# Expert capacities at a pitch of 8 tokens instead of 32, in a fused attention and mixture-of-experts kernel

## The chip, the cores and the metric

The kernel runs on one core of one Trainium2 chip. The metric is the time of one execution on the device, in microseconds (us). The engines are PE (TensorE, with its weight loads shown apart as PEld), DVE (VectorE), ACT (ScalarE), POOL (GpSimd) and SP (SyncE, which here only issues DMAs).

## What is computed

A windowed attention with sinks (4 batches, 8 heads, 768 positions, head size 64) gives 3072 tokens of 512 features. Each token picks one of 4 groups and one of the 4 experts in it, and goes through that expert alone:

```python
def _moe_ref(x, w_group, w_expert, w1, w2):
    ...
    g_idx = np.argmax(g_logits, axis=1)
    ...
        e_logits = xg @ w_expert[g]
        e_idx = np.argmax(e_logits, axis=1)
        ...
        for e in range(Eg):
            mask_e = e_idx == e
            if not mask_e.any():
                continue
            h = np.maximum(xg[mask_e] @ w1[g, e], 0.0)
            ye = h @ w2[g, e]
            combined = g_w[mask_g][mask_e] * e_w[mask_e]
            tok_idx = np.where(mask_g)[0][mask_e]
            out[tok_idx] = combined[:, None] * ye
```

`w1[g, e]` is 512x1024 and `w2[g, e]` 1024x512, in float32: 16 experts with 4 MB of weights each. `g_w` and `e_w` are the softmax weights of the group and the expert. How many tokens an expert gets is known only when the attention is done.

## The kernel before

The first part of the program is the attention, 128 queries at a time, with the routing worked out beside it on DVE. The second part runs the experts. They are ordered by how many tokens they hold, so an expert is named here by its **rank** r, from 0 (most tokens) to 15. A program without data-dependent loops needs a fixed number of places for each rank: the table `CAPT`. If an expert holds more tokens than its rank has places, `nov` is positive, and behind the main program a general path (`overflow`) runs the tokens that were left over, expert by expert, with nothing beside it.

Tokens are gathered from DRAM into tiles of 128 rows (`gather`), turned by PE so that features lie on partitions (`xpose`), and split into a high part, rounded to the format that PE takes in one pass (`F32R`), and a low part, the remainder. Weights are split in the same way in chunks of 128x1024: `whi` by a cast on ACT, `wlo` by a subtraction on DVE (`wjob`). A product is then three products: high by high, low by high, high by low. Both parts of the tokens stand side by side in one buffer: `xx` (before the first layer) and `hx` (before the second), the low part `T` columns behind the high part, T being the number of places.

`PARTS` lists the stages in the order in which they run (rank 0 first, then 1, 2, 2, 3 with 14, 8, 4 with 15, 9, 6 with 12, 5, 7 with 13, 10, 11). A stage has these forms:

- `layer1_wide` (T above 128): weights are stationary, tokens stream. For each of 8 blocks f of the hidden layer and 4 chunks c of the features: with T of 240 or more, three matmuls of T columns (a **triple**); below, `comb` is true and one matmul of 2T columns takes high and low together with `whi`, and one of T columns takes `wlo` (a **pair**).
- `layer1_narrow` (T up to 128): tokens are stationary, 512 weights stream; the hidden layer is then turned by PE (`hidden_t`).
- `layer2`: 128 tokens (or what is left of them) are stationary, 512 columns of `w2` stream, three matmuls for each of 8 blocks. Where the last tile holds at most 64 tokens (s > 0), its high and low parts stand next to each other and are loaded as one stationary operand.
- `few_tokens`: for the ranks in `FEW` (3, 4, 8, 9, 10, 11) the tokens above the last multiple of 128 (the **remainder**, `hq`) go through the second layer in plain float32, at 32 columns each, four matmuls side by side in the array. m is T without the remainder.
- `plain` (ranks 14 and 15): both layers in that way.

The order of all engines is fixed by the program text (`Pinned`). Between the matmuls, `spend(us)` counts an estimated time and emits weight jobs (`wjob`) and routing steps for ACT and DVE when enough of it has passed; the estimate of a block in `layer1_wide` is T/200 us and a constant. SP loads weight chunks ahead of that as buffers come free (`prefetch`). The results are scaled by ACT (`ot`) and written by an indirect DMA on POOL's queue (`scatter`).

Of the kernel before, what the change touches and what calls it, by code (L numbers as in the profile page):

```python
# [15 lines left out]
AF = mybir.ActivationFunctionType  # L16
ALU = mybir.AluOpType
# [5 lines left out]
P = 128  # L23
# [4 lines left out]
DM = H * D  # L28
# [14 lines left out]
XW = DM + GW  # L43
NEG = -1.0e30
BIG = 1 << 20
CAPT = [384, 256, 480, 288, 288, 224, 192, 192, 160, 160, 160, 160, 128, 128, 64, 32]
NTR = [(t + P - 1) // P for t in CAPT]
BASE = [sum(NTR[:r]) for r in range(NE)]
NCOL = sum(NTR)
# [19 lines left out]
MAXT = N // P  # L69
PARTS = [[dict(r=0, j0=0, T=EC * P, last=False), dict(r=0, j0=EC, T=CAPT[0] - EC * P, last=True)]]  # L70
for _g in GROUPS:
    if CAPT[_g[0]] > 3 * P:
        PARTS.append([dict(r=_g[0], j0=0, T=2 * P, last=False)])
        PARTS.append([dict(r=_g[0], j0=2, T=CAPT[_g[0]] - 2 * P, last=True)])
    else:
        PARTS.append([dict(r=r, j0=0, T=CAPT[r], last=True) for r in _g])
for _g in PARTS:
    _o = 0
    for _q in _g:
        _rem = _q["T"] % P  # L80
        _m = _q["T"] - _rem if _q["r"] in FEW else _q["T"]
        _q.update(o=_o, nt=(_q["T"] + P - 1) // P, s=_rem if _rem <= 64 and _m == _q["T"] else 0, plain=_q["T"] <= 64, m=_m)
        _o += 0 if _q["plain"] else 2 * _q["T"]
MAXB = 6
MAXA = 7
MAXO = MAXT + NE
# [48 lines left out]
def moe_attention(tc, kqT, vN, vS, nsw, wgx, w1, w2, out):  # L135
    nc = Pinned(tc)
    v = nc.vector
    with ExitStack() as top, ExitStack() as att:
# [18 lines left out]
        wz = const([P, 192], BF16, "wz")  # L157
        nc.gpsimd.memset(wz, 0.0)

        W = max(sum(2 * q["T"] for q in g if not q["plain"]) for g in PARTS)  # L160
        un = cp.tile([P, (NDC + NFC) * W], F32R, name="un")
        kb = wk.tile([P, 1 + 2 * NT, HP, BW], F32, name="kb", bufs=1)
        qb = wk.tile([P, NQ, HP, P], F32, name="qb", bufs=1)
        xx = un[:, 0:NDC * W].rearrange("p (c w) -> p c w", w=W)
        hx = un[:, NDC * W:(NDC + NFC) * W].rearrange("p (f w) -> p f w", w=W)
        dif = gp.tile([P, P], I32, name="xg")
# [146 lines left out]
        def late_consts():  # L313
# [8 lines left out]
            for r in range(NE):  # L322
                nc.gpsimd.memset(capt[:, r:r + 1], float(CAPT[r]))
                nc.gpsimd.memset(caps[:, r:r + 1], float(CAPT[r] // P))
# [151 lines left out]
        start = const([P, NE], F32, "start")  # L476
# [344 lines left out]
        po = ob[1].rearrange("p (c n) -> p c n", c=HP)  # L821
# [118 lines left out]
            v.tensor_copy(gate[0:w], src[0:w, DM:DM + 1])  # L940

        def split_h(q, fs, src):
            T, o, s, m = q["T"], q["o"], q["s"], q["m"]
            hi = hx[:, fs, o:o + m]
            nc.scalar.activation(hi, src[..., 0:m], AF.Relu)
            dve(0.1 + T / 960)
            yield
            if m < T:
                v.tensor_scalar(q["hq"][:, fs], src[..., m:T], 0.0, None, ALU.max)
            for a, z, d in ((0, m - s, m + s), (m - s, m, s)):  # L950
                if z > a:
                    v.scalar_tensor_tensor(hx[:, fs, o + a + d:o + z + d], src[..., a:z], 0.0,
                                           hi[..., a:z].bitcast(F32), ALU.max, ALU.subtract)
# [52 lines left out]
        def side_by_side(out, w, n, k, xs, ws, chunk, plain=True):  # L1006
            m = P // w
            for k0 in range(0, n, m):
                kk = range(k0, min(n, k0 + m))
                for c in kk:  # L1010
                    for a in range(m):
                        nc.tensor.matmul(out[a * w:(a + 1) * w, 0:k], xs(c), ws(c)[:, a * k:(a + 1) * k], start=c == 0, stop=c == n - 1)
                for c in kk:
                    held.pop(chunk(c), None) if chunk(c) != chunk(c + 1) else None
                prefetch(RAW + RAWB)
                if n == NFC and not plain:
                    pop_todo()
                yield 0.46 * k * m / 512 * len(kk) * w / 64
# [52 lines left out]
            yield from few_tokens(q, spare(), q["h"], q["T"], 0)  # L1071

        def few_tokens(q, po, h, T, jj):
            r, k = q["r"], DM * T // P
            yield from side_by_side(po, T, NFC, k, lambda f: h[:, f],
                                    lambda f: whole(2, r, f // 2)[:, (f % 2) * DM:(f % 2 + 1) * DM], lambda f: (2, r, f // 2), q["plain"])
            c = cg[r, jj]
            ot = yp.tile([P, DM], F32, name="ot", bufs=3)
            for a in range(P // T):
                nc.scalar.activation(ot[0:T, a * k:(a + 1) * k], po[a * T:(a + 1) * T, 0:k], AF.Copy, scale=c[0:T])  # L1080
            scatter(r, jj, T, ot)

        def scatter(r, jj, w, ot):
            cc = BASE[r] + jj
            nc.gpsimd.indirect_dma_start(
                out=outs[cc], out_offset=bass.IndirectOffsetOnAxis(ap=sidx[0:w, cc:cc + 1], axis=0),
                in_=ot[0:w], in_offset=None, bounds_check=N - 1, oob_is_err=False)

        def layer2(q, j):
            T, o, s, r, m = q["T"], q["o"], q["s"], q["r"], q["m"]  # L1090
            w = min(P, T - j * P)
            st = w if j * P + w > T - s else 0
            po = ps_o.tile([P, DM], F32, name="po")
            lastj = (j + 1) * P >= m
            end = q is PARTS[-1][-1] and j == 0
            rest = rest_of(q) if m < T and j == 0 else None
            pb = [spare(), po] if end else None
            for u, f in [(u, f) for u in range(2) for f in range(NFC)] if end else []:
                us = slice(f % 2 * DM + u * DM // 2, f % 2 * DM + (u + 1) * DM // 2)
                whi, wlo = (t[:, us] for t in weights(2, r, f // 2))  # L1100
                hh, hl = (hx[:, f, k:k + w] for k in (o, o + m + s))
                a, z = f == 0, f == NFC - 1
                nc.tensor.matmul(pb[u][:, 0:DM // 2], hh, whi, start=a, stop=False)
                nc.tensor.matmul(pb[u][:, 0:DM // 2], hh, wlo, start=False, stop=False)
                nc.tensor.matmul(pb[u][:, 0:DM // 2], hl, whi, start=False, stop=z)
                yield 0.36
                if rest and u == 0 and z:
                    yield from rest
            for f in range(0 if end else NFC):
                whi, wlo = (t[:, (f % 2) * DM:(f % 2 + 1) * DM] for t in weights(2, r, f // 2))  # L1110
                hh = hx[:, f, o + j * P:o + j * P + w]
                a, z = f == 0, f == NFC - 1
                if st:
                    hb = hx[:, f, o + j * P:o + j * P + 2 * w]
                    if z:
                        nc.tensor.matmul(po[0:w], hh, wlo, start=False, stop=False)
                    nc.tensor.matmul(po[0:2 * w], hb, whi, start=a, stop=z)
                    if not z:
                        nc.tensor.matmul(po[0:w], hh, wlo, start=False, stop=False)
                else:  # L1120
                    hl = hx[:, f, o + m + s + j * P:o + m + s + j * P + w]
                    nc.tensor.matmul(po[0:w], hh, whi, start=a, stop=False)
                    nc.tensor.matmul(po[0:w], hh, wlo, start=False, stop=False)
                    nc.tensor.matmul(po[0:w], hl, whi, start=False, stop=z)
                pop_todo()
                state["freed"] += 1 if q["last"] and lastj and f % 2 else 0
                yield 0.467 if st else 0.7
                if rest and f == 3:
                    yield next(rest)
            jj = q["j0"] + j  # L1130
            ot = yp.tile([P, DM], F32, name="ot", bufs=3)
            c = cg[r, jj]
            if end:
                for u in range(2):
                    nc.scalar.activation(ot[:, u * DM // 2:(u + 1) * DM // 2], pb[u][:, 0:DM // 2], AF.Copy, scale=c)
            else:
                nc.scalar.activation(ot[0:w], po[st:st + w], AF.Copy, scale=c[0:w])
            if st:
                v.scalar_tensor_tensor(ot[0:w], po[0:w], c[0:w], ot[0:w], ALU.mult, ALU.add)
            scatter(r, jj, w, ot)  # L1140
            if rest and not end:
                yield from rest

        def rest_of(q):
            po = spare()
            yield from few_tokens(q, po, q["hq"], 32, q["j0"] + q["nt"] - 1)

        def fetch(nxt):
            for q in nxt:
# [31 lines left out]
        for i in range(NI + 2):  # L1181
            live = i < NI
            a, b = i - 1, i - 2
# [385 lines left out]
```

## Time and profile before

| | us |
|---|---|
| median of 3 timed runs (lowest, highest) | 497.98 (496.86, 499.21) |
| the profiled execution | 493.82 |
| its span, first to last instruction | 492.0 |
| PE busy in the span | 479.8 |
| PEld / DVE / ACT / POOL busy | 412.4 / 350.8 / 331.2 / 157.2 |

The profiled execution is 1.8 us longer than its span. It lies 4.2 us (0.8%) under the median of the timed runs, which were separate executions.

### The profile page before, as it was taken

The numbers are of one execution on the slowest core, as the hardware profiler recorded it, in microseconds if no ns is written. First come the engines' busy times: TensorE is split into PE (matmuls) and PEld (weight loads), VectorE is DVE, ScalarE is ACT, GpSimd is POOL, SyncE is SP. The second block draws the span as 40 slices with busy tenths as digits, with TensorE's granted clock in tenths as the row PEclk, the third lists the DMA queues.
The fourth block names the chain that finished last, engine by engine and source line by source line (L and its number), as shares of the span: only waits on it lengthen the run. The fifth ranks groups of instructions, "written<-read, shape, count | busy, mean of one in ns | idle before, by whom it ended". The sixth has DMA issues, their size and how long they took to land.

```text
span 492.0 us, 15335 instructions
## 1 busy us (share of the span) xinstructions
PE 479.8 (98%) x5769; PEld 412.4 (84%) x5769; DVE 350.8 (71%) x1140; ACT 331.2 (67%) x878; POOL 157.2 (32%) x286
## 2 busy tenths in 40 slices
PE   8999999999999999999999999999999999999995
PEld 6788888888888888989888779797889788988894
DVE  7676888888988789973174157464788887788970
ACT  4898888889984355762264186646788777687861
POOL 3663563563573022322303042102402260105021
PEclk9999999999999999999999999999999999999999
DMA  7876767877876469894124389659959997768100
GB/s 215 248 229 225 260 228 227 253 254 263 286 254 212 131 227 387 289 316 148 68 70 142 113 291 385 208 180 329 391 180 386 399 394 238 280 212 292 61 28 28
DMA packets 50002, 114.75 MB, mean 233 GB/s; under 512 B 9486, under 2 KB 9486, under 8 KB 49920
## 3 DMA queue, kind: packets, MB, share of 16 engines
q1 hardware_dynamic: 45424, 100.14, 60.0%
q0 software_dynamic: 4352, 13.26, 7.5%
q8 instruction: 47, 0.77, 0.6%
q10 hardware_dynamic: 144, 0.29, 0.3%
q14 instruction: 35, 0.29, 0.2%
HBM read 100.89 MB, written 13.24 MB: 232 GB/s over the span
## 4 chain that ended last, share of the span: by engine, by line
PE 77%; DVE 7%; issue 7%; ACT 5%; POOL 1%; DMA 1%; POOLq 0%; DVEq 0%; ACTq 0%
PE po L105 34%; PE ph L105 28%; PE tp L105 7%; PE ps L105 6%; PE lg L105 3%; DVE wlo L105 2%; ACT pt L105 1%; ACT whi L105 1%; DVE sm L105 1%; DMA ni<-in_nsw 1%; POOL out L105 1%; DVE un L105 1%; DVE ps L105 1%; DVE xt L105 0%; ACT ot L105 0%
## 5 line engine op out<-in xcount | busy, mean ns | idle before, releaser
L105 DVE TENSOR_TENSOR wlo<-rw,whi 128x1024 fp32r<-128x1024 f32 x112 | 134.5, 1223 | 32.7 <-ACT whi L105 32.1
L105 PE MATMUL ph<-un,whi 128*128 128x256 f32 (+4 forms) x576 | 132.0, 316 | 1.4 <-DVE hc L105 0.8
L105 PE MATMUL po<-whi,un 128*128 128x512 f32 (+2 forms) x384 | 126.7, 395 | 0.0
L105 ACT CAST whi<-rw 128x1024 fp32r<-128x1024 f32 (+1 forms) x116 | 115.2, 1020 | 8.5 <-PE po L105 5.1
L105 POOL DMA_INDIRECT out<-ot,sidx x33 | 41.2, 1248 | 225.3 <-ACT ot L105 156.5
L105 PE MATMUL ph<-un,wlo 128*128 128x160 f32 (+4 forms) x416 | 100.6, 267 | 0.0
L105 PEld LDWEIGHTS ph<-un,whi 128*128 128x128 f32 x576 | 94.2, 189 | 3.8 <-DVE hc L105 1.3
L105 PEld LDWEIGHTS po<-whi,un 128*128 128x128 f32 (+1 forms) x384 | 70.8, 186 | 19.4 <-issue 2.6
L105 ACT ACTIVATE pt<-sm,st 128x136 f32<-128x136 f32 x192 | 76.0, 399 | 14.9 <-DVE st L105 14.8
L105 PE MATMUL po<-wlo,un 128*128 128x512 f32 (+3 forms) x200 | 78.0, 390 | 0.0
L105 PEld LDWEIGHTS ph<-un,wlo 128*128 128x128 f32 x416 | 77.0, 189 | 1.0
L105 DVE CUSTOM_DVE_ANT_0 sm<-ps,msk 128x136 f32<-128x136 f32 x192 | 45.7, 296 | 4.9 <-PE ps L105 1.9
L105 POOL DMA_INDIRECT xg<-xd,gidx x33 | 36.9, 1118 | 35.6 <-DVE idz L105 24.5
L105 PEld LDWEIGHTS po<-wlo,un 128*128 128x128 f32 (+2 forms) x200 | 36.3, 182 | 7.7
L105 DVE TENSOR_TENSOR hc<-ph,hc 128x160 f32<-128x160 f32 (+2 forms) x64 | 22.0, 346 | 26.4 <-ACT hc L105 26.1
L105 PE MATMUL ps<-kb,qb 64*64 64x216 f32 (+1 forms) x768 | 39.4, 339 | 0.8 <-DVE st L105 0.5
L105 ACT ACTIVATE un<-ph 128x256 fp32r<-128x256 f32 x40 | 15.4, 385 | 36.0 <-PE ph L105 35.6
L105 ACT ACTIVATION_READ_ACCUMULATOR pt<-sm,st 128x1 f32 x192 | 36.3, 189 | 0.0
L105 ACT ACTIVATE ot<-po,cg 128x512 f32<-128x512 f32 (+3 forms) x25 | 17.0, 680 | 27.6 <-PE po L105 27.5
L105 ACT COPY hc<-ph 128x160 f32<-128x160 f32 (+2 forms) x64 | 19.8, 312 | 19.0 <-PE ph L105 15.0
L105 PEld LDWEIGHTS ps<-kb,qb 64*64 64x64 f32 x768 | 26.4, 132 | 7.0 <-issue 1.0
L105 POOL TENSOR_SCALAR_AFFINE_SELECT pu<-pa 64x512 f32<-64x512 f32 x40 | 27.1, 676 | 12.0 <-ACT pa L105 11.9
(220 smaller groups left out, 737.9 us busy)
## 6 DMA issues: line engine op xcount, KB each, us to landing
rw<-in_w SPq DMA_DIRECT2D x128, 512.0 KB, 5.8
vv<-in_vN SPq DMA_DIRECT2D x24, 512.0 KB, 4.5
kb<-in_kqT SPq DMA_DIRECT2D x23, 288.0 KB, 4.5
qb<-in_kqT SPq DMA_DIRECT2D x24, 256.0 KB, 3.8
xd<-xt SPq DMA_DIRECT2D x24, 256.0 KB, 3.1
svr<-in_vS SPq DMA_DIRECT2D x4, 192.0 KB, 5.3
xg<-xd,gidx POOLq DMA_INDIRECT x33, 6.2
out<-ot,sidx POOLq DMA_INDIRECT x33, 5.8
```

The lines of the kernel that those rows point to most:

```text
L105: r = f(*a, **k)
```

## The change

Nine of the 16 ranks get fewer places: the table's numbers, multiples of 32 before, are now multiples of 8. With this case's inputs the ranks hold the numbers of tokens in the second row, counted with the reference:

| rank | 0 | 1 | 2 | 3 | 4 | 5 | 6 | 7 | 8 | 9 | 10 | 11 | 12 | 13 | 14 | 15 |
|---|---|---|---|---|---|---|---|---|---|---|---|---|---|---|---|---|
| tokens | 382 | 244 | 475 | 275 | 270 | 204 | 188 | 163 | 157 | 156 | 150 | 134 | 108 | 92 | 54 | 20 |
| places before | 384 | 256 | 480 | 288 | 288 | 224 | 192 | 192 | 160 | 160 | 160 | 160 | 128 | 128 | 64 | 32 |
| places after | 384 | 248 | 480 | 280 | 272 | 208 | 192 | 168 | 160 | 160 | 152 | 136 | 112 | 96 | 64 | 32 |

Reads of PSUM by ACT and DVE start at partitions 0, 32, 64 or 96 in this program. Rank 7's last tile now holds 40 tokens, so its low part is kept 64 columns behind the high part (`gap`), with 24 columns of it belonging to neither. Remainders of 24, 16 and 8 tokens keep their places at a pitch of 32 (`out[a * w:a * w + xs(c).shape[-1]]`).

```diff
-CAPT = [384, 256, 480, 288, 288, 224, 192, 192, 160, 160, 160, 160, 128, 128, 64, 32]
+CAPT = [384, 248, 480, 280, 272, 208, 192, 168, 160, 160, 152, 136, 112, 96, 64, 32]
...
-        _q.update(o=_o, nt=(_q["T"] + P - 1) // P, s=_rem if _rem <= 64 and _m == _q["T"] else 0, plain=_q["T"] <= 64, m=_m)
-        _o += 0 if _q["plain"] else 2 * _q["T"]
+        _s = _rem if _rem <= 64 and _m == _q["T"] else 0
+        _q.update(o=_o, nt=(_q["T"] + P - 1) // P, s=_s, gap=64 if _s else 0, plain=_q["T"] <= 64, m=_m)
+        _q["wid"] = 0 if _q["plain"] else 2 * _q["T"] + _q["gap"] - _s
+        _o += _q["wid"]
...
         def split_h(q, fs, src):
-            T, o, s, m = q["T"], q["o"], q["s"], q["m"]
+            T, o, s, m, gap = q["T"], q["o"], q["s"], q["m"], q["gap"]
...
-                v.tensor_scalar(q["hq"][:, fs], src[..., m:T], 0.0, None, ALU.max)
-            for a, z, d in ((0, m - s, m + s), (m - s, m, s)):
+                v.tensor_scalar(q["hq"][:, fs, 0:T - m], src[..., m:T], 0.0, None, ALU.max)
+            for a, z, d in ((0, m - s, m + gap), (m - s, m, gap)):
...
         def side_by_side(out, w, n, k, xs, ws, chunk, plain=True):
...
-                        nc.tensor.matmul(out[a * w:(a + 1) * w, 0:k], xs(c), ws(c)[:, a * k:(a + 1) * k], start=c == 0, stop=c == n - 1)
+                        nc.tensor.matmul(out[a * w:a * w + xs(c).shape[-1], 0:k], xs(c), ws(c)[:, a * k:(a + 1) * k], start=c == 0, stop=c == n - 1)
...
         def few_tokens(q, po, h, T, jj):
-            r, k = q["r"], DM * T // P
+            r, k, w = q["r"], DM * T // P, h.shape[-1]
...
-                nc.scalar.activation(ot[0:T, a * k:(a + 1) * k], po[a * T:(a + 1) * T, 0:k], AF.Copy, scale=c[0:T])
-            scatter(r, jj, T, ot)
+                nc.scalar.activation(ot[0:w, a * k:(a + 1) * k], po[a * T:a * T + w, 0:k], AF.Copy, scale=c[0:w])
+            scatter(r, jj, w, ot)
...
         def layer2(q, j):
-            T, o, s, r, m = q["T"], q["o"], q["s"], q["r"], q["m"]
+            T, o, s, r, m = q["T"], q["o"], q["gap"], q["r"], q["m"]
             w = min(P, T - j * P)
-            st = w if j * P + w > T - s else 0
+            st = s if j * P + w > T - q["s"] else 0
...
-                    hb = hx[:, f, o + j * P:o + j * P + 2 * w]
+                    hb = hx[:, f, o + j * P:o + j * P + st + w]
...
-                    nc.tensor.matmul(po[0:2 * w], hb, whi, start=a, stop=z)
+                    nc.tensor.matmul(po[0:st + w], hb, whi, start=a, stop=z)
```

The numbers of matmuls, weight chunks, gathers and scatters stay the same, and so does the width of the token buffers (`W` is set by rank 0). What changes in the instruction streams is the size of the tiles, and, because `spend` counts the smaller T, the places of a few weight jobs.

On PE, at the start of rank 11's first layer (`ph` is its accumulator, `un` the tokens, `hq` the remainder of rank 10 that is finished just ahead), before:

```order
L105 MATMUL ph<-rw,hq 32x128 x16
L105 MATMUL ph<-un,whi 128x320
L105 MATMUL ph<-un,wlo 128x160
L105 MATMUL ph<-un,whi 128x320
L105 MATMUL ph<-un,wlo 128x160
L105 MATMUL ph<-un,whi 128x320
L105 MATMUL ph<-un,wlo 128x160 x2
L105 MATMUL ph<-un,whi 128x320 x2
```

and now:

```order
L107 MATMUL ph<-rw,hq 24x128 x16
L107 MATMUL ph<-un,whi 128x272
L107 MATMUL ph<-un,wlo 128x136
L107 MATMUL ph<-un,whi 128x272
L107 MATMUL ph<-un,wlo 128x136
L107 MATMUL ph<-un,whi 128x272
L107 MATMUL ph<-un,wlo 128x136 x2
L107 MATMUL ph<-un,whi 128x272 x2
```

The sequence is the same; the streamed widths fall from 320 and 160 columns to 272 and 136, and the stationary remainder from 32 columns to 24.

Also on PE, where rank 7's second tile ends in the second layer and rank 13's tile begins (`po` is the accumulator, the first number the tokens that are stationary), before:

```order
L105 MATMUL po<-whi,un 128x512
L105 MATMUL po<-wlo,un 64x512
L105 MATMUL tp<-ident,xg 128x128 x4
L105 MATMUL tp<-ident,xg 128x32 x4
L105 MATMUL po<-wlo,un 64x512
L105 MATMUL po<-whi,un 128x512 x2
L105 MATMUL po<-wlo,un 128x512
L105 MATMUL po<-whi,un 128x512 x2
```

and now:

```order
L107 MATMUL po<-whi,un 104x512
L107 MATMUL po<-wlo,un 40x512
L107 MATMUL tp<-ident,xg 128x128 x4
L107 MATMUL tp<-ident,xg 128x24 x4
L107 MATMUL po<-wlo,un 40x512
L107 MATMUL po<-whi,un 104x512
L107 MATMUL po<-whi,un 96x512
L107 MATMUL po<-wlo,un 96x512
```

Again nothing has moved: 512 columns stream in each matmul as before, and the stationary operand is narrower (64 to 40, 128 to 104, 128 to 96).

On DVE, in rank 1's first layer, where the last steps of the routing run between the splits of weights (`wlo`) and of the hidden layer (`un`), before:

```order
L105 TENSOR_SCALAR inc<-inc 128x1
L105 TENSOR_TENSOR inc<-inc,gen 128x1
L105 CAST geni<-inc 128x1
L105 TENSOR_TENSOR inc<-inc 128x1
L105 TENSOR_TENSOR wlo<-rw,whi 128x1024
L105 SCALAR_TENSOR_TENSOR un<-ph,un 128x256
L105 CAST novi<-inc 128x1
L105 SCALAR_TENSOR_TENSOR un<-ph,un 128x256
L105 TENSOR_TENSOR wlo<-rw,whi 128x1024
```

and now:

```order
L107 TENSOR_SCALAR inc<-inc 128x1
L107 TENSOR_TENSOR inc<-inc,gen 128x1
L107 TENSOR_TENSOR wlo<-rw,whi 128x1024
L107 SCALAR_TENSOR_TENSOR un<-ph,un 128x248
L107 CAST geni<-inc 128x1
L107 TENSOR_TENSOR inc<-inc 128x1
L107 SCALAR_TENSOR_TENSOR un<-ph,un 128x248
L107 CAST novi<-inc 128x1
L107 TENSOR_TENSOR wlo<-rw,whi 128x1024
```

One split of a weight chunk (`wlo`) has moved ahead of two small routing steps and another behind the next two tiles; one more moves by one place in rank 4's first layer. On SP three weight loads of rank 3 now stand behind register loads (`eidi`, expert numbers) that stood between them. POOL's order is unchanged.

## Rows read from the trace of the kernel before

**Rows 1.** The page: span, busy time by engine (share of span), instructions.

```profile
span 492.0 us, 15335 instructions
...
PE 479.8 (98%) x5769; PEld 412.4 (84%) x5769; DVE 350.8 (71%) x1140; ACT 331.2 (67%) x878; POOL 157.2 (32%) x286
```

**Rows 2.** PE's waits, whole span: us in total, times, longest us.

```profile
PE tp L105 <- ACT pa L105: 1.3, 2, 0.7
...
PE ph L105 <- DVE hc L105: 0.8, 2, 0.4
```

**Rows 3.** Stretches: length; busy us PE, PEld, DVE, ACT, POOL; clock, DMA, GB/s.

```profile
225.00:250.00 25.00, 25.00 (x148) 22.26 (x147) 6.76 (x20) 7.56 (x20) 4.38 (x5) 1.00 0.18 62
...
350.00:375.00 25.00, 24.18 (x206) 21.35 (x206) 20.57 (x53) 20.22 (x46) 7.12 (x6) 1.00 0.78 288
375.00:400.00 25.00, 25.00 (x125) 20.45 (x124) 21.66 (x34) 20.12 (x31) 7.11 (x4) 1.00 1.04 396
```

**Rows 4.** PE timeline, triples: first and last of 32 (256, 288 tokens).

```profile
217.09 0.40 PE L105 MATMUL ph<-un,whi 128*128 128x256 f32 x2
...
228.09 0.40 PE L105 MATMUL ph<-un,whi 128*128 128x256 f32 x2
...
263.37 0.43 PE L105 MATMUL ph<-un,whi 128*128 128x288 f32 x2
...
275.72 0.43 PE L105 MATMUL ph<-un,whi 128*128 128x288 f32 x2
```

**Rows 5.** PE timeline, pairs: a stage's first row and the next's (224, 192, 160).

```profile
240.45 0.37 PE L105 MATMUL ph<-un,whi 128*128 128x448 f32 x1
...
250.53 0.39 PE L105 MATMUL po<-whi,un 128*128 128x512 f32 x1
...
421.02 0.34 PE L105 MATMUL ph<-un,whi 128*128 128x384 f32 x1
...
430.17 0.39 PE L105 MATMUL ph<-whi,un 128*128 128x512 f32 x1
...
452.47 0.31 PE L105 MATMUL ph<-un,whi 128*128 128x320 f32 x1
...
460.75 0.40 PE L105 MATMUL po<-whi,un 128*128 128x512 f32 x1
```

**Rows 6.** PE's weight loads by shape: columns loaded, busy us, mean ns.

```profile
L105 PEld LDWEIGHTS ph<-un,whi 128*128 128x128 f32 x576 | 94.2, 189 | 3.8 <-DVE hc L105 1.3 <-DVE un L105 0.7 <-ACT ot L105 0.2
...
L105 PEld LDWEIGHTS po<-whi,un 128*96 128x96 f32 x32 | 5.2, 161 | 2.1
...
L105 PEld LDWEIGHTS ph<-rw,hq 128*32 128x32 f32 x384 | 9.8, 109 | 3.4 <-issue 2.9 <-PE po L105 0.4
```

**Rows 7.** PE timeline, second layer: stationary of 128 tokens, then of 96.

```profile
232.52 0.39 PE L105 MATMUL po<-whi,un 128*128 128x512 f32 x1
...
239.52 0.39 PE L105 MATMUL po<-whi,un 128*128 128x512 f32 x1
...
258.34 0.39 PE L105 MATMUL po<-whi,un 128*96 128x512 f32 x1
...
262.46 0.39 PE L105 MATMUL po<-whi,un 128*96 128x512 f32 x1
```

**Rows 8.** PE timeline, transposes of 128 columns, then of 32.

```profile
441.36 1.03 PE L105 MATMUL tp<-ident,hs 128*128 128x128 f32 x8
...
312.28 0.43 PE L105 MATMUL tp<-ident,xg 32*128 32x32 f32 x4 [0.23 <-DVE cg L105]
```

**Rows 9.** PE timeline, the last remainder (32 tokens, four side by side).

```profile
480.98 1.96 PE L105 MATMUL ph<-rw,hq 128*32 128x128 f32 x64
```

**Rows 10.** Timeline of the end, all engines.

```profile
485.59 0.28 PE L105 MATMUL po<-whi,un 128*128 128x256 f32 x1
...
486.65 0.99 POOL L105 DMA_INDIRECT out<-ot,sidx  x1 [1.02 <-ACT ot L105]
```

**Rows 11.** The page: loads of one weight chunk, count, KB, us to landing.

```profile
rw<-in_w SPq DMA_DIRECT2D x128, 512.0 KB, 5.8
```

More of the change, by code (lines that the diff above doesn't have):

```diff
@@ L158, in moe_attention @@
         nc.gpsimd.memset(wz, 0.0)
-        W = max(sum(2 * q["T"] for q in g if not q["plain"]) for g in PARTS)
+        W = max(sum(q["wid"] for q in g) for g in PARTS)
         un = cp.tile([P, (NDC + NFC) * W], F32R, name="un")
@@ L1145, in rest_of @@
             po = spare()
-            yield from few_tokens(q, po, q["hq"], 32, q["j0"] + q["nt"] - 1)
+            yield from few_tokens(q, po, q["hq"][:, :, 0:q["T"] - q["m"]], 32, q["j0"] + q["nt"] - 1)
         def fetch(nxt):
```

## The prediction

> **What bounds the kernel now.** I read the engine totals first: PE is busy 479.8 us of a span of 492.0, 98%, the other engines 71% or less [rows 1]. Such a share is an average, so next come PE's own waits: the longest group in the whole run sums to 1.3 us, and in the expert half only one matters, 0.8 us in two waits for DVE's `hc` [rows 2]. The stretches show the same by time: PE is busy 25.00 us of 25 from 225 to 250 us and from 375 to 400 us, the second with DMA at its fullest (396 GB/s) and DVE and ACT at 21.66 and 20.12 us; the one stretch with a gap, 350 to 375 us, has 24.18 [rows 3]. The granted clock is 1.00 there, that is 2.4 GHz. So in the expert half a microsecond of PE work taken away is a microsecond off the end, as long as DVE and ACT keep up. Behind PE's last matmul (485.59 us) come only one scaling and one scatter (486.65 us) and its landing [rows 10]; the change touches none of these.
>
> What I must find is therefore how much PE time the smaller T saves. It isn't columns over clock, since each matmul also loads its own stationary operand.
>
> **The change, part by part.** *Triples (ranks 1, 3, 4).* With 256 tokens 31 triples take 228.09 - 217.09 = 11.00 us, 354.8 ns each; with 288 tokens 275.72 - 263.37 = 12.35 us, 398.4 ns [rows 4]. That is 43.6 ns for 32 tokens, 1.36 ns per token and triple, and a layer has 8 x 4 = 32 triples: 43.6 ns per token. Rank 1 loses 8 tokens, rank 3 loses 8, rank 4 loses 16: 0.35 + 0.35 + 0.70 = 1.40 us. For rank 1 this extrapolates below 256; a matmul there would take 354.8/3 - 8 x 0.454 = 114.6 ns. The weight load puts a floor under that: loads of 128, 96 and 32 columns take 189, 161 and 109 ns [rows 6], so 0.83 ns per column and some 107 ns for the 128 columns themselves, the rest being latency. 114.6 is still above, so I count the whole 0.35; its bounds are 0 and 0.35.
>
> *Pairs (ranks 5, 7, 10, 11).* A stage with T = 224 takes 250.53 - 240.45 = 10.08 us, with 192 430.17 - 421.02 = 9.15 us, with 160 460.75 - 452.47 = 8.28 us [rows 5]. Over 8 blocks that is 1.260, 1.144 and 1.035 us per block: 3.63 ns per token between 192 and 224, 3.40 between 160 and 192. A block streams 12 columns per token, so 12 columns cost no more than 8 would at the triples' 0.454 ns (3.63): the short matmul of a pair (160 columns, 73 ns) hides under the load for the next one, and only the long one gets cheaper. So: rank 5, 16 tokens x 3.63 x 8 = 0.46 us; rank 7, 24 x 3.40 x 8 = 0.65; rank 10, 8 x 3.40 x 8 = 0.22; rank 11, 24 x 3.40 x 8 = 0.65. Together 1.98 us. Rank 11 ends at 1.035 - 24 x 0.0034 = 0.953 us per block, above eight loads of 107 ns (0.856), so the floor isn't reached there by this sum; if it lies higher than I think, ranks 10 and 11 give nothing (0.87 us less).
>
> The layers' terms sum to 3.38 us. A page of the Trainium skill would have it larger: "TensorE: Matmul & The Clock Gate", section "Back-to-back issue gap", gives an isolated matmul N/2.4 ns and a constant; 104 tokens x 96 columns would then save 9984/2.4 = 4.16 us, an estimate from that page. The same section says that in a stream the spacing is set by load and matmul together, and this case's trace agrees with that half: 3.4 ns per token and block in the pairs, where streaming all 12 columns at 2.4 GHz would give 5.0.
>
> *Transposes.* Eight of 128 columns take 1.03 us, four of 32 take 0.43 us [rows 8]: 129 and 108 ns, 0.22 ns per column. The cut tiles have 152 tokens less, four transposes each, and ranks 12 and 13 turn 48 tokens less in eight: 992 columns, 0.22 us; at the triples' 0.454 ns it would be 0.45. I take 0.3.
>
> *Narrower stationary operands (second layer of ranks 1, 5, 7; both layers of 12 and 13).* The 512 streamed columns stay. Ten triples with 128 stationary tokens take 7.00 us, six with 96 take 4.12 us [rows 7]: 233.3 and 228.9 ns per matmul, 0.14 ns per token. Matmuls times tokens cut: 24x8 + 24x16 + 16x24 + 48x16 + 48x32 = 3264, so 0.45 us; below it nothing, since four nanoseconds are little to build on. I take 0.3.
>
> *Remainders of 24, 16 and 8 tokens.* 64 records of 128 columns take 1.96 us, 31 ns each [rows 9], too fast for one after another: four run side by side, and the time is that of the streamed weights. Narrower operands leave it: 0.
>
> *The gap of 64 columns in rank 7.* As many matmuls with as many streamed columns; `split_h` writes as much: 0.
>
> *Moved weight jobs.* No chunk changes places with another. Three loads of rank 3 go behind register loads on SP; these weights are needed from 263.37 us on [rows 4], and from 225 to 250 us the DMA moves 62 GB/s, with DVE busy 6.76 us of 25 [rows 3]: that idleness hides the delay. Without it, a load's 5.8 us to landing [rows 11] would be late. The split that moves in rank 1 (DVE) and the one in rank 4 pass small steps only: 0, with 0.5 us either way as bounds.
>
> Sum: 3.38 + 0.3 + 0.3 = 4.0 us; bounds 2.2 (floor higher, no side gains) and 4.3. From the profiled execution that is 493.8 - 4.0 = 489.8 us. That execution lies 4.2 us under the median of the timed runs, and the saving is a stretch of PE work common to both, so I take it off the median: **494.0 us**.
>
> **The rivals.** *1. The waits come back.* DVE and ACT are above 20 us of 25 from 350 to 400 us, and in this part of the program PE already waited 0.8 us for `hc` [rows 2, 3]. Weight splits don't shrink with T. If each of the four shortened pair stages got such waits, 3.2 us would go and 497.2 be left. Against it: from 375 to 400 us PE has no gap at the same load, and the copies and splits of DVE and ACT shrink with T too.
>
> *2. The weight loads bound more.* If nothing is saved below 256 columns in a triple and 160 tokens in a pair, and nothing in transposes and narrow operands, 0.35 + 0.87 + 0.6 us go: 2.2 are left, 495.8 us. For it speaks that the pairs' saving per token already falls from 3.63 to 3.40.
>
> *3. The remainders no longer run side by side (slower).* All rows are of 32 stationary columns; none is of 24, 16 or 8. If a group narrower than 32 took the array alone, each 1.96 us would be four times that, 5.9 more in each of ranks 3, 4, 10 and 11: 23.5 us, and 517.5 in all. One rank alone would outweigh the 4.0. Against it only the 96-token tiles speak, which run no slower than full ones [rows 7]. The Trainium skill's "TensorEngine Tiling (Array Packing)", section "Restrictions", asks only that the active columns don't exceed the tile's limit; no run here has shown that yet.
>
> *4. A rank overflows.* Counted with the reference, ranks 4, 10, 11 and 0 have 2 places to spare. Three tokens more in one of them, by rounding, would start the general path: 4 MB of weights at 396 GB/s [rows 3], at least 10.6 us with nothing beside it, 504.6 or more.
>
> **How the numbers follow.** Forecast 0.75, rival 1 0.08, rival 2 0.11, rival 3 0.03, rival 4 0.02, something else 0.01. A change under 0.5% (2.5 us) can't be told from none here, as the timed runs spread over 2.4 us. The forecast lies beyond that: faster 0.75; rivals 1 and 2 stay within it, with half of the rest: same 0.20; slower 0.05. The forecast's own range is 2.8 to 4.3 us with 1.2 us of scatter between medians: 492.5 to 496.4. To take in rival 2 with its scatter I go to 497.0, and below to 491.5, in case all 12 columns of a pair block count at the triples' rate (5.4 ns per token instead of 3.4 to 3.6, 1.2 us more), with the scatter: 491.5 to 497.0.
>
> **What would show it.** The stage of rank 11 should take about 7.6 us instead of 8.28, rank 7's 8.5 instead of 9.15, a triple of 248 tokens 344 ns. If pairs of 136 stay near 1.03 us per block, rival 2 holds; if PE's waits for `hc` or `un` grow by microseconds, rival 1; if the 64 records of the last remainder spread over 7 us, rival 3; if instructions follow the last scatter, rival 4. The prediction is wrong if PE's busy time doesn't fall by 3 to 4.3 us, or if it does and the span doesn't follow.

## Result, and the profile after

The changed kernel takes 492.27 us (median of 22 runs, 488.30 to 495.29), the kernel before 497.28 us in the same call (22 runs, 493.53 to 502.75): a ratio of 0.990, 95% interval [0.987, 0.992], so 5.1 us less (3.9 to 6.3). Forecast were 494.0 us (491.5 to 497.0), 4.0 less.

The profiled executions show only 1.4 us of this: 493.82 before, 492.45 now (1.3 between their spans). The page of the profile after, span and PE's line, answers to [rows 1]:

```profile
span 490.7 us, 15334 instructions
...
PE 476.5 (97%) x5769; PEld 407.1 (83%) x5769; DVE 348.1 (71%) x1140; ACT 328.8 (67%) x878; POOL 156.6 (32%) x286
```

PE's busy time fell by 3.3 us, the span by 1.3: PE now stands still where it did not before. By the prediction's last sentence that is a sign of being wrong (busy time falls by 3 to 4.3 us and the span doesn't follow), so it has to be explained. PE's waits, which answer to [rows 2], say where (us in total, times, longest us):

```profile
PE ph L107 <- issue: 1.6, 5, 0.4
...
PE ph L107 <- DVE un L107: 0.7, 1, 0.7
```

The wait for `hc` is gone, and one for "issue" has come, time in which the engine waited for nothing that the profile shows. PE's timeline after (start, length, operation, idle time before it) gives both the stages that the change shortens and the place of the new wait:

```profile
194.50 0.40 PE L107 MATMUL ph<-un,whi 128*128 128x248 f32 x2
...
202.43 0.39 PE L107 MATMUL ph<-un,whi 128*128 128x248 f32 x2
202.85 0.38 PE L107 MATMUL ph<-un,wlo 128*128 128x248 f32 x1
...
264.19 0.42 PE L107 MATMUL ph<-un,whi 128*128 128x280 f32 x2
...
276.07 0.42 PE L107 MATMUL ph<-un,whi 128*128 128x280 f32 x2
...
316.99 0.52 PE L107 MATMUL ph<-un,whi 128*128 128x272 f32 x2
...
328.76 0.41 PE L107 MATMUL ph<-un,whi 128*128 128x272 f32 x2
...
340.10 1.48 PE L107 MATMUL ph<-rw,hr 128*32 128x128 f32 x41
341.90 0.42 PE L107 MATMUL ph<-rw,hr 128*32 128x128 f32 x4 [0.32 <-issue]
342.63 0.47 PE L107 MATMUL ph<-rw,hr 128*32 128x128 f32 x5 [0.31 <-issue]
343.39 0.38 PE L107 MATMUL ph<-rw,hr 128*32 128x128 f32 x2 [0.28 <-issue]
344.14 0.38 PE L107 MATMUL ph<-rw,hr 128*32 128x128 f32 x2 [0.38 <-issue]
344.86 0.61 PE L107 MATMUL ph<-rw,hr 128*32 128x128 f32 x10 [0.33 <-issue]
345.40 0.50 PE L107 MATMUL po<-whi,un 128*128 128x512 f32 x1
...
421.83 0.32 PE L107 MATMUL ph<-un,whi 128*128 128x336 f32 x1
...
430.36 0.63 PE L107 MATMUL ph<-whi,un 128*96 128x512 f32 x2
...
469.21 0.39 PE L107 MATMUL ph<-un,whi 128*128 128x272 f32 x1
...
470.44 0.34 PE L107 MATMUL ph<-un,whi 128*128 128x272 f32 x1
...
476.08 0.34 PE L107 MATMUL ph<-un,whi 128*128 128x272 f32 x1
...
476.84 0.28 PE L107 MATMUL ph<-whi,un 128*128 128x256 f32 x1
...
479.76 1.93 PE L107 MATMUL ph<-rw,hq 128*8 128x128 f32 x64
```

The same places in the first profile of before, rank 15, rank 9 and rank 11:

```profile
340.49 1.96 PE L105 MATMUL ph<-rw,hr 128*32 128x128 f32 x64
342.38 0.50 PE L105 MATMUL po<-whi,un 128*128 128x512 f32 x1
...
348.07 0.31 PE L105 MATMUL ph<-un,whi 128*128 128x320 f32 x1
...
355.50 0.41 PE L105 MATMUL ph<-un,whi 128*128 128x320 f32 x1 [0.45 <-DVE hc L105]
...
357.67 0.39 PE L105 MATMUL po<-whi,un 128*128 128x512 f32 x1
...
469.64 0.42 PE L105 MATMUL ph<-un,whi 128*128 128x320 f32 x1
...
478.06 0.28 PE L105 MATMUL ph<-whi,un 128*128 128x256 f32 x1
```

Read against [rows 4, 5, 9] and these: 31 triples of 280 tokens take 276.07 - 264.19 = 11.88 us, 383.2 ns each (398.4 at 288), of 272 tokens 11.77 us, 379.7 ns. Rank 7's stage takes 8.53 us (9.15), rank 11's 7.63 (8.42; the 8.28 of [rows 5] are rank 10's). The 64 records of rank 11's remainder, now 8 columns wide, still take 1.9 us.

At 340.10 stands the second layer of rank 15, 64 short records that the change does not touch. In the first profile of before they took 1.89 us in one piece; here the first 41 run so, and then 2 to 5 come every 0.75 us: the stage takes 5.30 us. The next first layer, of rank 9, takes 8.24 us instead of 9.60, since PE no longer waits for `hc` there. Set side by side from stage start to stage start, before (first profile) to after, the rows give: the work that the change takes away -4.5 us, rank 15's stage +3.4, rank 9's -1.4, rank 6's first layer +0.1, a stall in rank 1's first layer +0.3 (it shows behind 202.43), and the attention up to 155 us +0.75, of which 0.53 are one more "issue" wait at 39 us. That is -1.3, as the spans differ. The other stages that the change doesn't touch agree within 0.02 us.

So there were two readings. **Theory:** the fixed saving is 4.5 us, and the shortage at rank 15 belongs to both kernels; the first profile of before happened to miss it. **Rival:** the change brings the shortage about, the saving is 4.5 less 2, and the timed 5.1 is something else.

### The profile page after: what moved, and what is told of

Its sections match the earlier page's. It is cut to its first block, busy times and chain, and to the rows that moved or that the text cites. A ratio compares the mean times of both kernels' runs of the same rounds, so it can differ in the third digit from the quotient of the medians.

```text
span 490.7 us, 15334 instructions
## 1 busy us (share of the span) xinstructions
PE 476.5 (97%) x5769; PEld 407.1 (83%) x5769; DVE 348.1 (71%) x1140; ACT 328.8 (67%) x878; POOL 156.6 (32%) x286
## 4 chain that ended last, share of the span: by engine, by line
PE 77%; issue 7%; DVE 6%; ACT 4%; DMA 2%; POOL 2%; POOLq 0%; DVEq 0%; ACTq 0%
PE po L107 34%; PE ph L107 29%; PE tp L107 6%; PE ps L107 5%; PE lg L107 2%; ACT pt L107 2%; DVE sm L107 1%; DMA ni<-in_nsw 1%; POOL out L107 1%; DMA qb<-in_kqT 1%; DVE un L107 1%; DVE wlo L107 1%; DVE ps L107 1%; ACT whi L107 1%; ACT pa L107 1%
## 5 line engine op out<-in xcount | busy, mean ns | idle before, releaser
L107 PE MATMUL ph<-un,whi 128*128 128x256 f32 (+9 forms) x576 | 128.3, 312 | 0.7 <-DVE un L107 0.7
L107 PE MATMUL po<-whi,un 128*128 128x512 f32 (+6 forms) x384 | 126.5, 395 | 0.0
L107 PE MATMUL ph<-un,wlo 128*128 128x160 f32 (+10 forms) x416 | 99.4, 264 | 0.0
L107 PEld LDWEIGHTS po<-whi,un 128*128 128x128 f32 (+5 forms) x384 | 69.7, 183 | 20.4 <-issue 2.6
L107 PE MATMUL po<-wlo,un 128*128 128x512 f32 (+7 forms) x200 | 77.9, 390 | 0.0
L107 PEld LDWEIGHTS po<-wlo,un 128*128 128x128 f32 (+6 forms) x200 | 35.7, 178 | 8.2
L107 DVE TENSOR_TENSOR hc<-ph,hc 128x160 f32<-128x160 f32 (+6 forms) x64 | 21.4, 338 | 26.0 <-ACT hc L107 23.7
L107 ACT ACTIVATE ot<-po,cg 128x512 f32<-128x512 f32 (+7 forms) x25 | 17.0, 680 | 26.3 <-PE po L107 26.1
L107 ACT COPY hc<-ph 128x160 f32<-128x160 f32 (+6 forms) x64 | 19.4, 304 | 19.1 <-PE ph L107 14.7
L107 PE MATMUL po<-pa,vv 128*64 128x64 f32 x768 | 31.1, 223 | 0.8 <-issue 0.5
```

The source lines that it names most:

```text
L107: r = f(*a, **k)
```

## The experiments

Each is the changed kernel with one edit, if nothing else is said. Stage times are from PE's timeline, from a stage's first row to the next stage's.

**1. The changed kernel again** (`after_again`, no edit).

> The changed kernel once more, unchanged, for a second profile. Theory (PE work per stage falls by fixed terms, and a random part comes from PE running short of instructions): the first-layer stages take the same times as in the first profile to within 0.1 us (rank 3 12.37, rank 4 12.24, rank 5 9.63, rank 7 8.53, rank 10 8.05, rank 11 7.63 us), while the 3.4 us that PE lost in rank 15's second layer (64 short records, marked as waiting for nothing) lie elsewhere or are gone. Rival (that loss belongs to the change, for instance through weight loads issued at another moment): it stands in the same place again, with 2 us or more.

495.61 us. Every stage that the change shortens repeats within 0.01 us (rank 3 12.37, rank 7 8.53, rank 11 7.63). Rank 15's stage took 6.53 us and the one behind it 6.68 instead of 5.70: these two make 2.2 of the 3.1 us between the two spans, and the attention 0.8. So the shortage is no accident of one run of the changed kernel; whether it is the change's, this run can't say.

**2. Ranks 12 and 13 wide again** (`wide_only`).

```diff
-CAPT = [..., 152, 136, 112, 96, 64, 32]
+CAPT = [..., 152, 136, 128, 128, 64, 32]
```

> The change without ranks 12 and 13, which keep 128 places; the rest as changed. Theory: the first-layer stages of ranks 1, 3, 4, 5, 7, 10, 11 as in the changed kernel (3.6 us less than before in all), ranks 12 and 13 and their part of the second layer as before: some 0.6 us more than the changed kernel, 4 us less than before, ratio about 0.992. Rival (most of the gain sits in the narrow operands of ranks 12 and 13): 2 us less than before or under.

493.79 us (9 runs), ratio 0.991 [0.988, 0.994]. In the stages, ranks 12 and 13 get back 0.07 and 0.02 us in their first layers, 0.16 and 0.27 in the second, and 0.03 and 0.14 in the second layers of ranks 9 and 5, where PE turns their tokens: 0.7 in all. The timed medians can't tell so little, the stages can: narrower stationary operands and smaller transposes are worth 0.7 us in these two ranks, as the theory had it (0.6).

**3. A pitch of 2** (`pitch2`): all capacities are the tokens, rounded up to even numbers.

```diff
-CAPT = [384, 248, 480, 280, 272, 208, 192, 168, 160, 160, 152, 136, 112, 96, 64, 32]
+CAPT = [384, 244, 476, 276, 270, 204, 188, 164, 158, 156, 150, 134, 108, 92, 64, 32]
```

> All capacities at a pitch of 2, right above the counts: 244, 476, 276, 270, 204, 188, 164, 158, 156, 150, 134, 108, 92 for ranks 1 to 13. Theory (each token cut from a rank saves 43.6 ns in a triple stage and 27 to 29 ns in a pair stage, down to the loads of the stationary operand): 10 tokens less in triples and 26 in pairs give 0.44 + 0.73 us, with narrower operands 0.2: 1.4 us less than the changed kernel, ratio to before 0.987. Rival (PE's weight loads already bound the pairs of the changed kernel): only the triples' 0.4 us, ratio 0.989. Rival (rounding moves a token to another expert): the general path starts and the time rises by 10 us or more.

493.57 us (12 runs), ratio 0.989 [0.986, 0.992]: not to be told from the change itself. The fixed gain in the stages behind rank 1 is 0.9 us, less than expected. Rank 2 gives 0.22 us in its two parts, rank 5 0.14 for 4 tokens, rank 7 0.15, rank 3 0.11, ranks 6 and 8 to 10 some 0.08 each; rank 11 gives 0.01 for its two tokens, and rank 4 loses 0.05. Rank 1 runs without its stall, but 0.8 us come back just ahead of it, where PE waits for a gather.

**4. Ranks 12 and 13 as pairs** (`wide1213`): the same computation, with weights stationary and T of 112 and 96 streamed, to find where a pair stops getting cheaper.

```diff
-                elif q["T"] > P:
+                elif q["T"] > P or q["r"] in (12, 13):
```

> The changed kernel with ranks 12 (112 places) and 13 (96) through the first layer with weights stationary, in pairs of 224 and 112 columns and of 192 and 96, in place of tokens stationary. Theory (a matmul can start no sooner than some 110 ns after the one before, the load of 128 columns): eight matmuls a block at 110 ns, 7.0 us for either rank's first layer, so no gain from 112 to 96. Rival (the saving per token goes on at 3.4 ns per block): 6.97 us for rank 12 and 6.54 for rank 13.

499.33 us. PE's timeline of this run, one block of rank 12 (T = 112), one of rank 13 (T = 96) and a wait in the latter's stage:

```profile
381.01 0.32 PE L107 MATMUL ph<-un,whi 128*128 128x224 f32 x1
...
381.91 0.32 PE L107 MATMUL ph<-un,whi 128*128 128x224 f32 x1
...
435.45 0.32 PE L107 MATMUL ph<-un,whi 128*128 128x192 f32 x1
...
436.35 0.32 PE L107 MATMUL ph<-un,whi 128*128 128x192 f32 x1
...
440.11 0.36 PE L107 MATMUL ph<-un,whi 128*128 128x192 f32 x1 [0.16 <-DVE hc L107]
```

A block of 96 tokens takes 436.35 - 435.45 = 0.90 us, and one of 112 tokens takes 0.90 too. That is the floor: 8 matmuls at 112 ns on average, at either width (where PE's timeline lists them singly, starts follow each other by 0.17 and 0.06 us in turn, so the theory's 110 ns holds for the mean alone). Eight loads of 107 ns, worked out from [rows 6], would take 0.86; that the load sets the floor is likely by that, but no run varied it. Rank 11's 136 tokens, at 0.940 us a block (476.08 - 470.44, over 6), are close above it. Beside that, this form made PE wait for `hc`: the two stages took 8.29 and 8.15 us, where the narrow form takes 5.53 and 5.56, and the second layers, without the transposes, gave only 0.7 and 0.6 us back.

**5 and 6. The kernel before, twice more** (`before_a`, `before_b`, no edit).

> The kernel before once more, unchanged, for a second profile. In all five profiles of changed kernels so far PE runs short of instructions in rank 15's second layer (5.3 to 6.6 us for 64 records instead of 1.9), in the one profile of before it does not. Theory (the shortage is no part of the change; it hits both kernels, and the first profile of before was a lucky one, 3.4 us under that kernel's median): this profile shows it too, with 3 to 5 us, and a time near 497. Rival (the change brings it, by the shifted weight loads): 1.9 us again.

> The kernel before a third time, as the run before this one: theory 5 us or more for rank 15's 64 records, rival 1.9 us.

500.75 and 497.74 us. PE's timeline of the second, rank 15's second layer:

```profile
342.17 1.34 PE L105 MATMUL ph<-rw,hr 128*32 128x128 f32 x36
343.94 0.38 PE L105 MATMUL ph<-rw,hr 128*32 128x128 f32 x3 [0.43 <-issue]
...
346.91 0.66 PE L105 MATMUL ph<-rw,hr 128*32 128x128 f32 x13 [0.38 <-issue]
347.50 0.51 PE L105 MATMUL po<-whi,un 128*128 128x512 f32 x1
```

The same shortage: 347.50 - 342.17 = 5.33 us, and 5.73 in `before_a`, with 8.24 us for rank 9 behind it in both. The rival falls: the shortage belongs to both kernels. Of the ten profiles with these 64 records and full weight loads (of before, of the change and of its variants here) nine have it, with 5.30 to 6.56 us; only the first profile of before does not. Between `before_b` (span 496.0) and the change (490.7), which both have it, the spans differ by 5.3 us: 4.5 in the stages that the change shortens, 0.4 in a wait in rank 1 (below), and the rest in pieces of 0.2 or less.

**7. Rank 15 in half as many records** (`r15_two`): its second layer at a pitch of 64, two matmuls of 256 columns side by side in place of four of 128.

```diff
-            yield from few_tokens(q, spare(), q["h"], q["T"], 0)
+            yield from few_tokens(q, spare(), q["h"], 64, 0)
```

> The changed kernel with rank 15's second layer two side by side instead of four: 32 records of 256 columns in place of 64 of 128, so half as many instructions on PE for the same product. Theory (PE runs short of instructions because 128 of them, loads and matmuls, are used up in 1.9 us): at 32 records the shortage is gone, the stage takes 3.7 us where the changed kernel took 5.3 and 6.5, and the whole is 1.6 to 3.8 us less than the changed kernel. Rival (the shortage is set by the DMA traffic at that moment, whatever PE runs): the stage takes 3.7 us and the same 3.4 to 4.7 us loss, and the whole is 1.8 us more.

492.37 us (4 runs), ratio 0.989 [0.985, 0.994]. The timelines of PE, ACT and DVE, rank 15 and then a wait in rank 9:

```profile
340.29 3.65 PE L107 MATMUL ph<-rw,hr 128*32 128x256 f32 x32
343.87 0.50 PE L107 MATMUL po<-whi,un 128*128 128x512 f32 x1
...
352.04 1.05 ACT L107 CAST whi<-rw 128x1024 fp32r<-128x1024 f32 x1 [2.26 <-DMA rw<-in_w]
...
353.12 1.22 DVE L107 TENSOR_TENSOR wlo<-rw,whi 128x1024 fp32r<-128x1024 f32 x1 [1.71 <-ACT whi L107]
...
354.64 0.41 PE L107 MATMUL ph<-un,whi 128*128 128x320 f32 x1 [0.79 <-DVE hc L107]
```

No "issue" gap: 3.58 us instead of 5.30. But rank 9 now takes 9.29 us instead of 8.24, as PE comes earlier and waits for DVE's `hc`. The rows show why: ACT waits 2.26 us for a weight chunk to land, DVE's split waits for ACT, and `hc` stands behind that split. Of 1.7 us taken away 1.05 come back one stage later, and the whole can't be told from the change, where 1.6 to 3.8 us less were expected.

**8. A rank that overflows** (`overflow11`), for the price of rival 4.

```diff
-CAPT = [..., 160, 160, 152, 136, 112, 96, 64, 32]
+CAPT = [..., 160, 160, 152, 132, 112, 96, 64, 32]
```

> The changed kernel with 132 places for rank 11, which holds 134 tokens, so that the general path runs for one tile. Price of rival 4 of the prediction: 4 MB of weights at 396 GB/s with nothing beside them, at least 10.6 us more; with the register loads, the list through DRAM and two layers in plain float32 I expect 40 to 70 us more. Should the general path cost under 5 us, the rival was priced wrongly.

547.86 us, 55.6 more than the change. PE's timeline behind the main program:

```profile
491.76 0.66 PE L1455 MATMUL tx<-ident,tabw 128*128 128x128 f32 x2 [6.38 <-DVEq L1342]
...
520.49 1.09 PE L1509 MATMUL tx<-ident,oxg 128*128 128x128 f32 x4 [24.75 <-DMA oxg<-xd,gi]
522.41 9.69 PE L1516 MATMUL oph<-w1s,oxT 128*128 128x512 f32 x16 [0.83 <-issue]
...
533.32 7.13 PE L1528 MATMUL opo<-w2s,ohT 128*128 128x512 f32 x16
```

For two tokens PE waits 24.75 us for their gather and works 17 us in plain float32. From 491.76 to 520.49 us, where PE was busy for 1.1 us, its granted clock was 0.50, that is 1.2 GHz, and in the first of the two layers 0.73 on average; the second, at 1.00, takes 7.13 us for as many matmuls, not 9.69. The prediction's bound of 10.6 us was a fifth of it.

**9 and 10. The change again, timed, and the two edits of 3 and 7 together** (`after_timed`, `both`).

> The changed kernel again, unchanged, timed beside the kernel before on the same chip as the run both. The fixed savings of PE work add up to some 4.5 us, so the ratio should come out near 0.990 (between 0.988 and 0.993), and rank 15's second layer should again take 5.3 to 6.6 us instead of 1.9 if the shortage of instructions is the rule there. If the 5.1 us measured first had been luck of the runs, the ratio would be nearer 0.993 (the 3.4 us of the layers' terms alone).

> The changed kernel with capacities equal to the tokens rounded up to the next even number (places of pitch2) and rank 15's second layer as 32 records of 256 columns (r15_two). If the two savings are independent, 0.85 us of fixed PE work and about 0.7 us net of the shorter stage and the wait that returns in rank 9 come off the changed kernel: some 1.5 us under it in the same call, ratio near 0.987. If the waits for hc grow as PE gets ahead of DVE, part of the 1.5 us is lost again: rank 9's stage would then be over 9.3 us.

The change: 493.03 us (12 runs) against 497.08 (17 runs), ratio 0.992 [0.989, 0.995]; 4.1 us less. With the 5.1 of the first call on either side, the stages' 4.5 us lie within both intervals. Rank 15's stage took 6.56 us again. `both`: 490.96 us (6 runs), ratio 0.987 [0.983, 0.992]. It is 2.1 us under the change in the same call and the lowest median of a kernel with all its work, but its interval overlaps that of the change. Its profile shows why not to add gains up: rank 15's stage is 3.58 us as in `r15_two`, and in rank 9 stands this row:

```profile
355.93 0.41 PE L107 MATMUL ph<-un,whi 128*128 128x312 f32 x1 [1.71 <-DVE hc L107]
```

Rank 9 takes 10.15 us, 1.9 more than in the change: in this execution all of rank 15's gain was given back.

**11 and 12. Half the weight traffic around rank 15** (`half_loads`, and once more as `half_loads_b`). What starves PE there? The second half of the split weights is made from the loaded half.

```diff
+        def cut(l, r):
+            return r in (9, 6, 12)
...
-                if l == 1:
+                if cut(l, r):
+                    src = w1[e, c * P:(c + 1) * P, 0:F // 2] if l == 1 else w2[e, 2 * c * P:(2 * c + 1) * P, :]
+                    nc.sync.dma_start(rw[:, 0:F // 2], src.rearrange("o p f -> (o p) f"))
+                elif l == 1:
...
+            if cut(l, r):
+                nc.scalar.copy(hi[:, 0:y], rw[:, 0:y])
```

> The changed kernel with the weights of ranks 9, 6 and 12 loaded by half (256 KB for each chunk in place of 512, the loaded half used twice, so the second half of these experts' weights is left out of the computation). Their loads are those in flight in rank 15's second layer, where the DMA moves 308 GB/s and PE runs short of instructions. If the traffic of the weight loads causes the shortage, the stage falls from 5.3 to 1.9 us, and rank 9's next first layer grows from 8.24 to about 9.6 us as in the profile of the kernel before, where PE waited for hc. If the shortage comes from something else (the place of these instructions in the program, or how many short ones come in a row), it stays at 5.3 to 6.6 us at half the traffic.

> The same kernel as half_loads once more, since one profile of the kernel before had no shortage by itself: one profile without it could be that chance, two would be unlikely (among the profiles with rank 15's 64 short records taken so far, one in ten had none).

488.05 and 489.59 us. PE's timeline of the first:

```profile
339.47 1.95 PE L107 MATMUL ph<-rw,hr 128*32 128x128 f32 x64
```

All 64 records in one piece in both runs, 1.88 and 1.89 us, by the same PE instructions as in the change. So the weight loads are the likely cause of the shortage. The stretches ahead of it (length; busy us PE, PEld, DVE, ACT, POOL; clock, DMA share, GB/s), of `half_loads`:

```profile
330.00:340.00 10.00, 10.00 (x130) 7.54 (x126) 3.28 (x7) 4.63 (x10) 0.82 (x1) 1.00 0.58 187
340.00:342.00 2.00, 2.00 (x56) 1.71 (x48) 1.50 (x4) 1.96 (x6) 1.60 (x2) 1.00 0.90 320
```

and of the change:

```profile
330.00:340.00 10.00, 10.00 (x122) 7.32 (x114) 3.32 (x5) 3.99 (x6) 0.19 (x1) 1.00 0.84 303
340.10:345.40 5.30, 3.68 (x66) 2.21 (x65) 2.83 (x5) 3.48 (x7) 4.38 (x4) 1.00 0.90 308
```

What differs is the 10 us ahead, 187 GB/s against 303; in the stage itself `half_loads` moves about as much as the change. How loads would hold PE's instructions up is not settled. The profile's page lists instructions among the DMA transfers (queue q8: 47 packets, 0.77 MB, in the change), beside the weights. But the one packet of that queue in the 10 us ahead of the stage took 0.95 us in the change and in both runs of `half_loads`, so a slow transfer there is not shown.

Nor do two runs exclude that they escaped as the first profile of before did. Both ran rank 1's first layer, 140 us earlier, in 11.03 us, without the stall that it has in the other runs with 248 places (at 244, `pitch2` has the shortage without it, but waits just ahead); the edit doesn't touch that stage, and the loads there were full (316 and 327 GB/s from 185 to 205 us). The first profile of before is the only one with 256 places that lacks the stall (11.30 us), and it is the one without the shortage. The edit also gives ACT and DVE 24 more instructions each, which no run separates from the loads.

The expectation for rank 9 was wrong: it took 8.24 us and did not wait for `hc`, though PE came to it 4 us earlier than in the change. That fits the rows of `r15_two`, where the wait for `hc` goes back to a weight load: with half as much to land, there was nothing to wait for.

## Why the prediction was right, step by step

- **What bounds it.** Right: what was taken from PE's work came off the end, as soon as profiles are compared that both have the shortage (`before_b` and the change: PE's busy time 5.2 us less, the span 5.3). The sign of being wrong that the first pair of profiles gave came from the first profile of before. Stages with no work taken away and no wait stayed within 0.02 us, but for rank 6's first layer (9.18 or 9.26 us in either kernel).
- **Triples** (predicted 1.40 us). Rank 3 -0.47 and rank 4 -0.71 (0.35 and 0.70), so the cost between 256 and 288 tokens is not a straight line: the first 8 tokens off saved 15.2 ns a triple, the next 8 3.5. Rank 1: 23 triples from 194.50 to 202.43, 344.8 ns each or 114.9 a matmul, where 114.6 was extrapolated; 0.3 us for 32 triples. The first profiles hide it (11.30 to 11.37), since this stage can stall, for "issue" or for DVE's `un`, by a length that changes from run to run: not at all in the first profile of before, 0.3 us in the change's, 0.8 in the two later runs of before (12.18 and 12.11), and not at all in the runs with half the loads (11.03 twice).
- **Pairs** (predicted 1.98). Rank 5 -0.43, rank 7 -0.62, rank 10 -0.23, as forecast within 0.03. Rank 11 gave 0.79 instead of 0.65: the step extrapolated 3.40 ns per token and block below 160, and measured were 4.2 (a block of 0.940 us, not 0.953). From 136 tokens to 112 only 0.04 us a block are left.
- **The layers together:** 3.55 us, with 3.38 predicted. By "TensorE: Matmul & The Clock Gate", section "Back-to-back issue gap" of the Trainium skill, N/2.4 ns for an isolated matmul, they would have saved 4.16, an estimate from that page; the traces bear out the other half of that section, that load and matmul set the spacing together: from 112 tokens to 96 nothing is saved, at 112 ns a matmul.
- **Transposes and narrow operands** (0.3 each). Undersized, 0.6 for 0.96: the second layers of ranks 6 and 12 gave 0.22, of 7 and 13 0.32, of rank 5 (where rank 13's tokens are turned) 0.20, first layers of 12 and 13 0.10, all others some 0.12. Both times I took a value between a low bound and the price at a row's own rate; the rows' higher prices, 0.45 for each, would have been right in sum. (The 129 ns for a transpose of 128 columns were a misreading of [rows 8]: the record of 1.03 us ends behind the start of the next matmul, which came 0.79 us after its own, 99 ns for each.) With it the fixed saving is 4.5 us, just above the upper bound of 4.3 that the sum gave itself.
- **Remainders, rival 3.** Fallen. PE's weight loads after, by shape (columns loaded, busy us, mean ns):

```profile
L107 PEld LDWEIGHTS ph<-rw,hq 128*24 128x24 f32 x128 | 3.2, 102 | 1.3 <-issue 0.9 <-PE po L107 0.4
...
L107 PEld LDWEIGHTS ph<-rw,hq 128*8 128x8 f32 x64 | 1.6, 90 | 0.1
L107 PEld LDWEIGHTS ph<-rw,hq 128*16 128x16 f32 x64 | 1.6, 96 | 0.5 <-issue 0.5
```

  Loads get shorter by 6 to 7 ns for 8 columns, and 32 records take 1.07 us at 24 and at 16 columns, 1.08 at 32: the width of the stationary remainder doesn't matter, and four still run at a time. The Trainium skill's "TensorEngine Tiling (Array Packing)", section "Restrictions", asks of the width only that the active columns don't exceed the tile's limit, and the trace agrees for 24, 16 and 8.
- **The gap and the moved jobs** (0). Right: no stage shows them; rank 3's first layer starts with no wait.
- **Rival 1, waits come back.** Not in the change, but its mechanism is real: 0.8 us in `r15_two` and 1.7 in `both` as soon as PE gets to rank 9 earlier. In the change the shortage at rank 15 covers it: PE reaches rank 9 later. The argument made against it, that DVE's and ACT's work shrinks with T, is not what kept it away.
- **Rival 2, the floor.** There is one, 0.90 us a block, but it lies below 136 tokens. A block of rank 11 took 0.940 us at 136 tokens, 0.937 at 134 (`pitch2`), 0.930 at 132 (`overflow11`) and 0.90 at the 112 and 96 of `wide1213`, so little is left to gain there, as `pitch2` found.
- **Rival 4.** It did not happen. Its price is 55.6 us, so two places to spare are an expensive bet if inputs change.
- **The base.** The step from the profiled execution to the median, a saving common to both, was right, and its reason is now known in the main: against the two later ones of before, that execution lacked the shortage (2.5 and 2.1 us net of rank 9), the stall in rank 1 (0.8 us) and the "issue" wait at 39 us (0.54). It was luck of that execution, and taking the saving off the median was the way round it.

## What to carry to other kernels

Price a cut in streamed columns from stages of neighbouring widths in the same trace, and ask at which width streaming less stops paying; here that was at 0.90 us a block, reached at 112 tokens, and below that a finer pitch bought nothing. Take the saving off the median and not off the profiled execution, and where two single profiles are compared, do it stage by stage: here 4.5 us of saving showed as 1.3. When PE gets faster ahead of a stage that hangs on weight loads, expect part of it back as a wait there.

## What the runs showed of the hardware

PE can run short of instructions with nothing in its way that the profile names: 64 records of 128 columns that run in 1.9 us took 5.3 to 6.6 us in nine of ten profiles, behind 10 us in which the DMA moved 301 to 314 GB/s, and 1.9 us in both runs with 185 GB/s there. As 32 records of 256 columns they took 3.6 us without a gap, behind 311 and 302 GB/s. The first profile of before, at 304 GB/s, escaped it once, so the traffic alone doesn't decide; what else does stays open, and so does whether the two runs at half the loads escaped by the loads or by chance.
